# Early loads of an attention kernel: packed query and key rows, v uncast on the sync queue, weights and filter ordered behind v, sines after the first exps

## The chip, the cores and the metric

The kernel runs on one core of one Trainium2 chip. The metric is the time of one execution in microseconds (us). All times below are device times of that core. Each run carries a state: fast, slow, or unknown for a kernel that was run only once. A profiled execution has a span, which is the part that the profile covers and is 1.8 to 2.1 us shorter than the time; spans are compared with spans and times with times.

Engines are named as the profile names them: PE is TensorE, PEld its weight load, DVE is VectorE, ACT is ScalarE, POOL is GpSimd, SP is SyncE, which here only issues DMAs. "A queue" is a stream of DMA work: one is filled by GpSimd, one by the sync engine, one can be filled by ScalarE. A "piece" is one contiguous run of bytes that a DMA engine moves; 16 DMA engines work for the core.

## The reference, cut to what matters

```python
# q, k, v: (4 batches, 8 heads, 768, 64) f32, scaled by 0.1; n_global = 8, n_local = 96
scores = q @ k^T / 8
keep   = (column < 8) or (0 <= row - column < 96)
bias   = -slope[head] * (96 if global and not local else |row - column|)
a      = softmax(scores + bias, masked by keep)
x      = a @ v                       # heads joined: (4, 768, 512)
x1, x2, x3 = split(x @ w_proj)       # w_proj: (512, 1536)
y      = x1 * irfft(rfft(x2) * rfft(filter)) * x3     # over the 768 positions
out    = y @ w_out                   # w_out: (512, 512)
```

The kernel builds the Fourier transform as matmuls with cosine and sine tables. It works on four batches one after the other. Attention of batch 0 cannot overlap with the convolution of an earlier batch, because there is none; so the start of the kernel is the place where TensorE can run dry.

## The kernel before: the parts that the change and the argument touch

The kernel records its operations with a model cost, what each reads and writes, and a bias. A greedy scheduler then orders them on a modelled clock, and the result is the program order of each engine. Two things follow for the reader. An order between two operations on the same engine is real. An order between two engines is real only where data dependences make one wait for the other; the framework inserts those waits, and the scheduler's clock inserts none.

```python
def load(self, eng, dst, src, w, nbytes, name, r=()):      # G: GpSimd's queue, S: the sync queue
    self.loads += 1
    e = {"G": self.nc.gpsimd, "S": self.nc.sync}[eng]
    return self.g.op(eng, ..., lambda _: e.dma_start(dst, src),
                     w=w, r=r, nbytes=nbytes, name=name, bias=-2000.0 + self.loads)

def load_q(self, b, t):                                    # 1024 pieces of 256 B
    src = self.q[b, :, P * t:P * t + P, :].rearrange("h p d -> p h d")
    if b == 0:    # f32 by the sync queue, then a cast on VectorE
        ...
    else:         # GpSimd's queue casts on the way
        self.load("G", self.qn[:, t], src, [("qn", t)], (1024, 256), f"q{t}")

def load_v(self, b, ts):
    ...
    for t in ts:
        self.load_rows(("vn", s), vt, self.v, b, t)        # GpSimd's queue, cast on the way
        ...                                                # global rows: SBUF copies on the sync queue

# eight mask exps, one a head, 648 columns each, after the sines
for h in range(self.H):
    g.op("A", act(648), lambda _, h=h: nc.scalar.activation(
        self.mask[:, h], dm.rearrange("p a b -> p (a b)"), Act.Exp, scale=-self.slopes[h]), ...)

def load_first(self):
    for c in range(3):
        for t in ([0, 1, 2], [3, 4], [5])[c]:
            self.load_q(0, t)
        for t in self.GRP[c]:
            self.load_rows(("kn",), self.kn, self.k, 0, t)
        if c == 0:
            self.distances()
        self.load_v(0, self.GRP[c])
    ...
    for o in (0, 256):
        self.load_w(o, 256)
        self.load_w(2 * self.DM + o, 256)
    self.load_w(self.DM, self.DM)
    self.load("G", self.fl, ...)                           # the filter
```

In each attention a head pair goes through scores (PE), two exps (ACT), a mask product (DVE), and value matmuls (PE) that read v.

The softmax here doesn't subtract the row's maximum and nothing guards it: scores larger than these inputs give would overflow.

## Time and profile before

| | before |
|---|---|
| time | 200.63 us, median of 3 runs (200.32 to 201.04) |
| span of the profiled run | 198.0 us |
| TensorE busy | 185.1 us of it |
| first exp of attention 0 | 20.91 us |
| value matmuls of the second head pair (the marker used below) | 23.64 us |
| first projection with w | 32.72 us |

The page of the kernel before gives the busy time of each engine, and in 40 slices of about 5 us the busy tenths of TensorE and its granted clock.

```profile
PE 185.1 (93%) x1654; PEld 109.7 (55%) x1654; DVE 151.0 (76%) x380; ACT 150.3 (76%) x305; POOL 75.7 (38%) x96
...
PE   7993699989999699999999999999999999999992
...
PEclk9998599999999969999999999999999999999999
```

The fourth and fifth digits are the hole: TensorE is full everywhere else but for one dip near 65 us. The windows of the kernel before show it in numbers. The columns are the stretch, its length, then busy us and instruction counts of PE, PEld, DVE, ACT and POOL, then granted clock, DMA share and GB/s.

```profile
15.00:20.00 5.00, 1.79 (x19) 0.83 (x15) 1.68 (x5) 4.99 (x8) 5.00 (x7) 0.83 1.44 98
20.00:25.00 5.00, 3.54 (x40) 2.66 (x39) 3.07 (x9) 5.00 (x12) 5.00 (x7) 0.50 1.79 153
...
30.00:40.00 10.00, 9.77 (x117) 6.48 (x115) 8.67 (x21) 5.33 (x13) 4.47 (x6) 1.00 1.81 182
```

TensorE waits for ScalarE there. The timeline of ScalarE before (start, length, engine, line, operation, tiles, count) says why: an exp table load, 5.17 us of mask exps, and only then the exps of the scores.

```profile
14.54 1.28 ACT L551 ACT_TABLE_LOAD   x1
15.83 5.17 ACT L551 ACTIVATE mask<-dm 128x648 f16<-128x648 f32 x8
20.91 6.80 ACT L645 ACTIVATE E<-bank 128x432 f16<-128x432 f32 x16
```

The timeline of GpSimd before shows that v comes ahead of w on the same queue: the last three v loads are issued at 17.30 us, and w only after them.

```profile
17.30 2.65 POOL L376 DMA_DIRECT2D vn<-in_v_dram  x3
19.89 3.78 POOL L376 DMA_DIRECT2D w<-in_moe_w_proj_dram  x5
```

After the hole TensorE is what bounds the kernel.

### The profile page before, as it was taken

The numbers are of one execution on the slowest core, as the hardware profiler recorded it, in microseconds if no ns is written. First come the engines' busy times: TensorE is split into PE (matmuls) and PEld (weight loads), VectorE is DVE, ScalarE is ACT, GpSimd is POOL, SyncE is SP. The second block draws the span as 40 slices with busy tenths as digits, with TensorE's granted clock in tenths as the row PEclk, the third lists the DMA queues.
The fourth block names the chain that finished last, engine by engine and source line by source line (L and its number), as shares of the span: only waits on it lengthen the run. The fifth ranks groups of instructions, "written<-read, shape, count | busy, mean of one in ns | idle before, by whom it ended". The sixth has DMA issues, their size and how long they took to land.

```text
span 198.0 us, 4444 instructions
## 1 busy us (share of the span) xinstructions
PE 185.1 (93%) x1654; PEld 109.7 (55%) x1654; DVE 151.0 (76%) x380; ACT 150.3 (76%) x305; POOL 75.7 (38%) x96
## 2 busy tenths in 40 slices
PE   7993699989999699999999999999999999999992
PEld 2571465755545486665455657654656665445640
DVE  5993599795599999898169999951998999159540
ACT  3889997384899987387698966857999975785852
POOL 8969983499889899085000100000000000000000
PEclk9998599999999969999999999999999999999999
DMA  7999999999999999999620400025000000214025
GB/s 156 214 152 96 152 184 209 158 157 144 147 167 156 154 154 161 108 69 148 223 110 0 30 0 0 5 106 212 3 2 3 0 3 0 106 53 159 3 108 211
DMA packets 90933, 20.90 MB, mean 106 GB/s; under 512 B 83776, under 2 KB 87840, under 8 KB 90912
## 3 DMA queue, kind: packets, MB, share of 16 engines
q0 software_dynamic: 80912, 12.52, 95.7%
q1 hardware_dynamic: 10000, 8.10, 12.6%
q8 instruction: 13, 0.21, 0.4%
q14 instruction: 8, 0.07, 0.1%
HBM read 26.61 MB, written 6.29 MB: 166 GB/s over the span
## 4 chain that ended last, share of the span: by engine, by line
PE 72%; DMA 10%; POOL 9%; DVE 4%; issue 2%; ACT 1%; POOLq 0%; ACTq 0%
PE bank L739 19%; PE bank L786 11%; PE bank L826 10%; PE bank L595 8%; PE bank L806 8%; DMA kn<-in_k_dram 5%; DMA w<-in_moe_w_proj_dram 5%; PE bank L633 4%; PE bank L677 3%; POOL vn L376 3%; PE bank L608 3%; PE bank L712 3%; POOL kn L376 3%; PE bank L682 2%; POOL w L376 1%
## 5 line engine op out<-in xcount | busy, mean ns | idle before, releaser
L739 PE MATMUL bank<-xT,w 128*128 128x384 f16 x256 | 44.1, 326 | 0.1
L645 ACT ACTIVATE E<-bank 128x432 f16<-128x432 f32 x96 | 42.7, 570 | 0.5 <-PE bank L633 0.3
L376 POOL DMA_DIRECT2D kn<-in_k_dram x28 | 25.2, 915 | 23.5 <-PE bank L608 17.8
L739 PEld LDWEIGHTS <-w 128*128 128x128 f16 x256 | 24.8, 98 | 16.9
L376 POOL DMA_DIRECT2D vn<-in_v_dram x28 | 25.2, 922 | 6.4 <-PE bank L682 5.2
L364 ACT ACTIVATE x<-bank 128x384 f16<-128x384 f32 x31 | 15.7, 508 | 15.4 <-PE bank L739 14.3
L656 DVE TENSOR_TENSOR E<-E,mask 128x864 f16<-128x864 f16 x32 | 18.6, 602 | 7.6 <-ACT E L645 7.3
L697 DVE TENSOR_TENSOR xn<-bank,rc 128x256 f16<-128x256 f32 (+1 forms) x48 | 22.5, 469 | 1.7
L826 PE MATMUL bank<-wo,y 128*128 128x512 f16 x96 | 22.4, 379 | 0.0
L747 DVE TENSOR_TENSOR g<-bank,x 128x384 f16<-128x384 f32 x32 | 17.3, 552 | 5.6 <-PE bank L739 5.2
L364 ACT ACTIVATE ot<-bank 128x512 f32<-128x512 f32 x24 | 14.3, 597 | 8.8 <-PE bank L826 8.8
L360 ACT CAST eo<-bank 128x384 f16<-128x384 f32 x31 | 14.7, 487 | 7.2 <-PE bank L806 6.8
L677 PE MATMUL bank<-vn,E 128*128 128x65 f16 x224 | 19.6, 201 | 0.1
L677 PEld LDWEIGHTS <-E 128*128 128x128 f16 x224 | 16.3, 103 | 4.9 <-DVE E L656 1.3
L682 PE MATMUL bank<-vn,E 128*128 128x65 f16 x192 | 19.1, 199 | 0.0
L806 PE MATMUL bank<-inv,X 128*128 128x384 f16 x96 | 18.7, 326 | 0.0
L595 PE MATMUL bank<-ab,fwd 128*128 128x512 f16 x72 | 18.3, 379 | 0.0
L376 POOL DMA_DIRECT2D qn<-in_q_dram x18 | 16.0, 913 | 2.2 <-PE bank L633 0.7
L633 PE MATMUL bank<-QT,KT 64*128 64x216 f16 (+2 forms) x224 | 15.9, 248 | 0.7 <-DVE inv L360 0.2
L608 PE MATMUL bank<-ident,kn 128*128 128x128 f16 x112 | 10.9, 231 | 5.8 <-ACT E L645 4.4
L682 PEld LDWEIGHTS <-E 128*128 128x128 f16 x192 | 14.7, 101 | 1.2
L826 PEld LDWEIGHTS <-y 128*128 128x128 f16 x96 | 9.4, 98 | 10.5
(103 smaller groups left out, 323.3 us busy)
## 6 DMA issues: line engine op xcount, KB each, us to landing
out_dram<-ot SPq DMA_DIRECT2D x24, 256.0 KB
kn<-in_k_dram POOLq DMA_DIRECT2D x24, 128.0 KB, 5.7
vn<-in_v_dram POOLq DMA_DIRECT2D x24, 128.0 KB, 6.2
qn<-in_q_dram POOLq DMA_DIRECT2D x18, 128.0 KB, 7.8
ot<-in_q_dram SPq DMA_DIRECT2D x6, 256.0 KB
w<-in_moe_w_proj_dram POOLq DMA_DIRECT2D x4, 256.0 KB, 6.5
g<-in_moe_filter_fft_dram POOLq DMA_DIRECT2D x1, 768.0 KB, 12.9
w<-in_moe_w_proj_dram POOLq DMA_DIRECT2D x1, 512.0 KB, 9.4
```

The source lines that it names most:

```text
L364: self.nc.scalar.mul(out, in_, c)
L376: return self.g.op(eng, 0.57 + 0.00035 * nbytes[0] if eng == "G" else 0.5, lambda _: e.dma_start(dst, src), w=w, r=r, nbytes=nbytes, name= ...
L595: self.nc.tensor.matmul(b.f32(), self.fwd[:, kt, s, :], src[i][:, kt, :], start=(kt == 0), stop=(kt == 2))
L633: nc.tensor.matmul(bs[hh].f32()[:, off:off + w], self.KT[hs, hp, P * m:P * m + P], self.QT[hs, hp, KL * m:KL * m + w], start=(off == 0), s ...
L645: g.op("A", act(432), lambda _, hh=hh: nc.scalar.activation(eo[:, hh], bs[hh].f32()[:, 0:432].rearrange("p (m w) -> p m w", m=2), Act.Exp, ...
L677: nc.tensor.matmul(o[:, hh, i], ef[:, at:at + P], vt[:, t, 2 * hp + hh, :], start=first, stop=(t == 0), skip_group_check=True)
L682: nc.tensor.matmul(o[:, hh, i], ef[:, at:at + P], vt[:, t - 1, 2 * hp + hh, :], start=False, stop=True, skip_group_check=True)
L697: nc.vector.tensor_mul(xn[:, ts[0]:ts[0] + nt].rearrange("p t h d -> p h t d"), o[:, :, :, 0:D], r.to_broadcast([P, 2, nt, D]))
L739: nc.tensor.matmul(bk.f32()[:, 0:h], self.w[:, c, o + P * j:o + P * j + P], self.xT[:, c, h * s:h * s + h], start=(c == 0), stop=(c == 3))
L786: nc.tensor.matmul(bk.f32(), src[:, c, P * t:P * t + P], w[:, c, DM:2 * DM], start=(c == 0), stop=(c == 3))
L806: nc.tensor.matmul(bk.f32()[:, 0:h], X[:, s, cs], self.inv[:, s, :], start=(s == slots[0]), stop=(s == slots[-1]))
L826: nc.tensor.matmul(bk.f32(), y[:, c, P * t:P * t + P], self.wo[:, c, :], start=(c == 0), stop=(c == 3))
```

## The change

The intent is to start attention 0 sooner. Queries and keys of batches 0 and 1 are loaded by head pair as six consecutive rows per partition: for the queries of a batch, four loads of 256 pieces of 1536 B in place of six loads of 1024 pieces of 256 B. w goes out in three loads in place of five. The masks are computed from 264 columns a head and spread by copies, in place of exps over 648. The sines, and their table load, go behind the first exps. v of batch 0 goes out uncast on the sync queue, into memory that is free at that time, and seven casts on ScalarE and VectorE bring it into place; the intent is to keep it apart from GpSimd's queue. The loads of w, of the filter and of batch 1 are declared as readers of v tiles, so that they come "behind v". The diff, cut to its core:

```diff
 def load_first(self):
-        for c in range(3):
-            for t in ([0, 1, 2], [3, 4], [5])[c]:
-                self.load_q(0, t)
-            for t in self.GRP[c]:
-                self.load_rows(("kn",), self.kn, self.k, 0, t)
-            if c == 0:
+        for hp in range(4):
+            self.load_pair("q", 0, hp)
+            self.load_pair("k", 0, hp)
+            if hp == 1:
                 self.distances()
-            self.load_v(0, self.GRP[c])
 ...
-        for o in (0, 256):
-            self.load_w(o, 256)
-            self.load_w(2 * self.DM + o, 256)
-        self.load_w(self.DM, self.DM)
+        self.first_v()
+        for o in (0, 2 * self.DM, self.DM):
+            self.load_w(o, self.DM, [("vn", 0, 4)])
         self.load("G", self.fl, ..., (768, 2048), "filter",
+                  [("vn", 0, 6)])

+    def first_v(self):
+        ...
+        for t in range(7):
+            st, ks = ...                       # a free buffer: h1, h2 or X, read as f32
+            for rows, n, src in ((slice(0, NG), NG, 0), (slice(NG, P), KL, self.K0[t])):
+                self.load("S", st[rows], self.v[0, :, src:src + n].rearrange("h p d -> p h d"),
+                          [("vst", t, n)], (8 * n, 256), f"v{t}")
+            g.op("AV", ..., lambda e, st=st, t=t: self.copy(e, vt[:, t, :, 0:self.D], st), ...,
+                w=[("vn", 0, t)], name="vcast")

+    def load_pair(self, what, b, hp):          # 256 pieces of 1536 B
+        hs = slice(2 * hp, 2 * hp + 2)
+        src = (self.q if what == "q" else self.k)[b, hs].rearrange("h (p t) d -> p h (t d)", t=6)
+        ...
+            self.load("G", self.packed(what)[:, hs], src, [(what + "p", hp)] + ..., (256, 1536), ...)

-        for h in range(self.H):
-            g.op("A", act(648), ...)           # a mask exp a head
+        for hp in range(4):
+            for h in (2 * hp, 2 * hp + 1):
+                for lo, hi, at in ((0, n, n), (n, n + 48, 600)):   # 216 and 48 columns
+                    g.op("A", act(hi - lo), ...)
+            ...                                # VectorE copies spread them

 def graph(self):
         self.setup()
-        self.tables()
         self.load_first()
         self.attention(0)
+        g.batch = (-10.0, 0.0)
+        self.tables()
 # cut: the transposes of packed rows, the distances, the scheduler's model of two DMA queues
```

## The prediction

> **What bounds the kernel now.** The engine summary has TensorE busy 185.1 of 198.0 us. By the busy-time windows it is dense from about 32 us to the end at a granted clock near 1.0; before that it is starved (1.79 us busy in 15 to 20, 3.54 in 20 to 25). In the timeline the first exp starts at 20.9 us, behind the distance mask (Pool until 14.7 us) and eight mask exps on ScalarE (5.17 us from 15.83). The chain of waits then runs through the w load (9.4 us, to 32.3) and a key load of batch 1 (9.9 us). The change acts on the start; my marker is the value matmuls of the second head pair (23.6 us). About 174 us follow it.
>
> **What it removes.** Query and key loads of batches 0 and 1 fall from 1024 pieces of 256 B to 256 of 1536 B per load. Mask exps fall from 648 to 264 columns a head (estimate 3.5 us for 5.2); sines leave the start. Without v, exps could begin near 13 us.
>
> **What it adds.** v of batch 0 goes to the SP queue uncast: 7168 pieces of 256 B, then seven casts (about 0.5 us each). Packed batch 1 needs 48 half-width transposes each for q and k, not 24 and 28: some 2 us of TensorE. A sine and an exp table load (1.28 us each) move into the middle.
>
> **The step that decides.** "Held behind v" is an order in the schedule's model only. In the instruction order Pool issues the three w loads without any wait, right after the `far` selects and one key load; the filter and batch 1 follow, waiting only for old slots and transposes. I expect w issued at 10 to 13 us and a Pool backlog from about 13 to 43 us, beside v on SP's queue. The Trainium skill, "DMA: Bandwidth & Descriptors", section on queues, rings and completion order, says each DMA engine alternates between queues packet by packet. The DMA packet records agree: alone, SP moves 1000 pieces of 256 B per us; [...]at 28.6 to 29.4 us SP's 1040 B pieces come every 0.14 us, one per 2 KB of w. So v gets about one 256 B piece per 2048 B w piece or 1536 B q/k piece on each engine (94 and 77 ns a pair, estimates from those rates). Then v tiles 0 and 1 land by 14 us, 2 about 20, 3 about 27, 4 about 33, 5 about 38, 6 about 46. The casts sit in order on ScalarE ahead of the exps (tiles 1 to 4) and on VectorE ahead of the first mask products (5, 6), so all of attention 0 waits.
>
> **Sum.** Marker 23.6 to about 47 us (+23); minus about 5 for weights and batch 1 already there, plus about 3 for transposes, tables and a cold clock: +18 to +21. Predicted 219 us, range 203 to 229. Chances: faster 0.15, same 0.09, slower 0.76.
>
> **What would show it.** In the timeline, w issued before 13 us; v casts ending long idle stretches on ScalarE and VectorE between 14 and 47 us; TensorE nearly empty there, dense after; w landed by 25 us.
>
> **What would make it wrong.** If the queues share by time or SP is favoured, v is in by about 24 us, attention 0 starts some 8 us sooner than before, and the time is 188 to 195. If Pool issues w late, v escapes most of the contention.

## The result, and the profile after

The changed kernel takes 224.91 us (median of 4 runs, 222.81 to 225.07), beside 200.8 us of the kernel before in the same rounds. The ratio is 1.118, with a 95% interval of 1.111 to 1.125. Here and below a ratio is the mean time of one kernel's fast runs over that of the other's of the same rounds, so it is not quite the ratio of the medians quoted. The prediction (slower, 219 us, range 203 to 229) was right.

The page after gives the same three lines as before.

```profile
PE 184.9 (83%) x1715; PEld 106.9 (48%) x1715; DVE 152.9 (68%) x390; ACT 156.8 (70%) x326; POOL 57.8 (26%) x79
...
PE   7590001129999999979999999999999999999993
...
PEclk9998555556999999999999999999999999999998
```

TensorE does the same amount of work (184.9 us beside 185.1). All that is new is a longer hole: six slices of about 5.6 us each are empty or nearly so. The windows after show it, in the columns explained above.

```profile
15.00:20.00 5.00, 1.63 (x34) 1.04 (x31) 3.55 (x15) 0.00 (x0) 2.91 (x4) 1.00 1.26 195
20.00:25.00 5.00, 0.54 (x4) 0.30 (x5) 2.31 (x8) 1.85 (x5) 1.28 (x2) 0.56 1.22 197
25.00:30.00 5.00, 0.00 (x0) 0.00 (x0) 1.48 (x5) 0.85 (x2) 0.82 (x2) 0.50 1.23 195
30.00:40.00 10.00, 1.42 (x11) 0.79 (x11) 0.00 (x0) 2.21 (x4) 4.78 (x6) 0.50 1.24 183
```

From 20 to 40 us no compute engine is busy for half of the time. Only the DMA works throughout, at 183 to 197 GB/s; before it was 98 and 153 GB/s in the first two of these stretches. The clock has fallen to 0.50, as "TensorE: Matmul & The Clock Gate" of the Trainium skill says in its Part 1 (the default state is throttled, and activity releases it); this trace agrees, with a mean of 0.50 from 25 to 50 us and 0.77 from 50 to 60. The low clock is a consequence here and not the cause: in the stretch from 25 to 30 us TensorE ran no instruction.

What the engines wait for is v. The waits view after, for the first 60 us (line, what it waited for, total us, times, longest us), begins with two lines:

```profile
DVE vn L366 <- DMA h<-in_v_dram: 24.4, 2, 19.3
ACT vn L366 <- DMA h<-in_v_dram: 23.2, 4, 7.8
```

The timelines after name the casts one by one. In brackets is the idle time before each and what ended it. ScalarE first, then VectorE:

```profile
21.62 0.62 ACT L366 CAST vn<-h 128x512 f16<-128x512 f32 x1 [7.80 <-DMA h<-in_v_dram]
29.14 0.62 ACT L366 CAST vn<-h 128x512 f16<-128x512 f32 x1 [5.67 <-DMA h<-in_v_dram]
35.84 0.62 ACT L366 CAST vn<-h 128x512 f16<-128x512 f32 x1 [5.38 <-DMA h<-in_v_dram]
...
41.90 0.62 ACT L366 CAST vn<-h 128x512 f16<-128x512 f32 x1 [4.31 <-DMA h<-in_v_dram]
```

```profile
45.78 0.43 DVE L366 CAST vn<-h 128x512 f16<-128x512 f32 x1 [19.31 <-DMA h<-in_v_dram]
46.13 0.60 DVE L735 TENSOR_TENSOR E<-E,mask 128x864 f16<-128x864 f16 x1
...
48.55 0.43 DVE L366 CAST vn<-X 128x512 f16<-128x512 f32 x1 [1.73 <-DMA X<-in_v_dram]
48.89 0.60 DVE L735 TENSOR_TENSOR E<-E,mask 128x864 f16<-128x864 f16 x1
```

Each engine runs in order, so a cast that waits for its tile holds the exps and mask products behind it, although these need no v. The value matmuls of the second head pair are the marker. The timelines of TensorE before and after:

```profile
23.64 0.29 PE L677 MATMUL bank<-vn,E 128*128 128x65 f16 x2
```

```profile
49.55 0.29 PE L756 MATMUL bank<-vn,E 128*128 128x65 f16 x2 [1.78 <-DVE E L735]
```

The marker moved by 25.9 us and the span by 25.2 us (223.2 beside 198.0). From the marker to the end it is 174.4 us before and 173.7 us after. So the whole loss is in the start.

v comes late because it shares the DMA engines with loads that the change meant to hold back. The timeline of GpSimd after, with nothing in brackets: no wait stands before w or the filter.

```profile
7.95 0.89 POOL L382 DMA_DIRECT2D kn<-in_k_dram  x1
8.83 2.24 POOL L382 DMA_DIRECT2D w<-in_moe_w_proj_dram  x3
11.04 0.86 POOL L382 DMA_DIRECT2D g<-in_moe_filter_fft_dram  x1
```

The queue view after, from 17 to 22 us, gives packets, MB (as written) and the share of engine time of each queue; q0 is GpSimd's, q1 the sync queue. Below it is the same view of the kernel before from 5 to 6 us, when both queues moved pieces of 256 B.

```profile
q0 software_dynamic: 795, 0.79, 93.6%
q1 hardware_dynamic: 695, 0.17, 26.7%
```

```profile
q0 software_dynamic: 908, 0.11, 170.7%
q1 hardware_dynamic: 275, 0.07, 34.1%
```

(The counts hold some packets of 4 bytes; the shares of overlapping packets add up to more than 100%.) After, the two queues take turns nearly piece by piece, 795 to 695, while a w piece is 2048 B read (1024 B written) and a v piece 256 B. v gets some 140 pieces per us from 17 to 28 us. The 908 to 275 of the kernel before is no ratio of turns, because the view adds up engines: from 5.2 to 5.6 us the records hold 39 sync pieces beside 406 of GpSimd's queue, and by their start times (the records name no engine) these 39 are only a few chains, some with a piece every 14 ns (about the pace of an engine that has sync pieces alone) and some with one every 39 ns. A count from the trace's DMA packet records, by size and microsecond, gives these rates (pieces per us, all 16 engines):

```
kernel and stretch            GpSimd's queue                      sync queue
before, 3 to 4 us             nothing                             256 B: about 1050
after, 17 to 22 us            2048 B read: about 155              256 B: about 135
after, 32 to 36 us            1536 B read: about 175              256 B: about 180
e1 (below), 13 to 15 us       256 B read, cast: about 394         256 B: about 387
```

The start times of one queue's pieces repeat with a step of 105 ns beside 2048 B, 86 ns beside 1536 B and 39 ns beside cast pieces of 256 B, and the other queue's pieces repeat with the same step where it was looked for (2048 B and 256 B). With 16 engines, these steps would make 152, 186 and 410 pairs per us, close to the counts: one piece of each queue in turn.

### The profile page after: what moved, and what is told of

It reads as the page before. It is cut to its first block, busy times and chain, and to the rows that moved or that the text cites. A ratio compares the mean times of both kernels' runs of the same rounds, so it can differ in the third digit from the quotient of the medians.

```text
span 223.2 us, 4576 instructions
## 1 busy us (share of the span) xinstructions
PE 184.9 (83%) x1715; PEld 106.9 (48%) x1715; DVE 152.9 (68%) x390; ACT 156.8 (70%) x326; POOL 57.8 (26%) x79
## 4 chain that ended last, share of the span: by engine, by line
PE 62%; SPq 16%; DVE 7%; ACT 6%; DMA 5%; issue 2%; DVEq 0%; ACTq 0%
PE bank L818 18%; SPq L382 16%; PE bank L910 9%; PE bank L870 9%; PE bank L634 7%; PE bank L890 5%; DMA X<-in_v_dram 5%; PE bank L710 3%; PE bank L756 3%; ACT E L723 2%; PE bank L791 2%; PE bank L761 2%; DVE E L735 2%; DVE xn L776 2%; PE bank L685 2%
## 5 line engine op out<-in xcount | busy, mean ns | idle before, releaser
L723 ACT ACTIVATE E<-bank 128x432 f16<-128x432 f32 x96 | 43.5, 556 | 4.9 <-PE bank L710 3.2
L710 PE MATMUL bank<-QT,KT 64*128 64x216 f16 (+2 forms) x224 | 17.2, 265 | 24.9 <-ACT QT L366 19.5
L382 POOL DMA_DIRECT2D vn<-in_v_dram x21 | 18.8, 897 | 51.7 <-PE bank L761 36.6
L710 PEld LDWEIGHTS <-KT 64*128 64x128 f16 x224 | 8.9, 99 | 32.9 <-issue 24.3
L756 PE MATMUL bank<-vn,E 128*128 128x65 f16 x224 | 19.0, 198 | 4.5 <-DVE E L735 4.5
L382 POOL DMA_DIRECT2D kn<-in_k_dram x22 | 18.9, 861 | 13.9 <-PE bank L685 5.8
L756 PEld LDWEIGHTS <-E 128*128 128x128 f16 x224 | 15.7, 100 | 11.0 <-DVE E L735 7.2
L366 ACT CAST vn<-h 128x512 f16<-128x512 f32 x4 | 2.5, 620 | 23.2 <-DMA h<-in_v_dram 23.2
L761 PE MATMUL bank<-vn,E 128*128 128x65 f16 x192 | 18.4, 196 | 0.0
L366 DVE CAST vn<-h 128x512 f16<-128x512 f32 x2 | 0.9, 454 | 24.4 <-DMA h<-in_v_dram 24.4
L382 POOL DMA_DIRECT2D qn<-in_q_dram x16 | 14.1, 879 | 13.5 <-DMA w<-in_moe_w_proj_dram 5.0
```

The lines of the kernel that those rows point to most:

```text
L382: return self.g.op(eng, 0.57 + 0.00035 * nbytes[0] if eng == "G" else 0.5, lambda _: e.dma_start(dst, src), w=w, r=r, nbytes=nbytes, name= ...
L710: nc.tensor.matmul(bs[hh].f32()[:, off:off + w], self.KT[hs, hp, P * m:P * m + P], self.QT[hs, hp, KL * m:KL * m + w], start=(off == 0), s ...
L723: g.op("A", act(432), lambda _, hh=hh: nc.scalar.activation(eo[:, hh], bs[hh].f32()[:, 0:432].rearrange("p (m w) -> p m w", m=2), Act.Exp, ...
L756: nc.tensor.matmul(o[:, hh, i], ef[:, at:at + P], vt[:, t, 2 * hp + hh, :], start=first, stop=(t == 0), skip_group_check=True)
L761: nc.tensor.matmul(o[:, hh, i], ef[:, at:at + P], vt[:, t - 1, 2 * hp + hh, :], start=False, stop=True, skip_group_check=True)
```

## The experiments

Nine kernels were run. Theory A: v of batch 0 is starved on the sync queue beside the large loads of GpSimd's queue, because nothing makes w wait for v; nothing else in the change costs much. Rivals: the loss comes from another part of the change (more transposes, later sines, packed rows, casts), or it is due to how the scheduler remade the order of everything else. Five kernels keep the changed kernel's order of compute on every engine (e1, e3, e4, e6, e9); they change only DMAs, waits and how many rows a cast covers. Three (e2, e5, e7) let the scheduler make a new order. b1 starts from the kernel before, and its order is new too.

### b1_vsp: the kernel before, with only v of batch 0 moved

```diff
 # kernel before, load_first
-            self.load_v(0, self.GRP[c])
+            self.first_v(self.GRP[c])     # as in the changed kernel: uncast, sync queue, then a cast a tile
```

> The kernel before with one part of the change alone: v of batch 0 uncast on SP's queue with seven casts; q, k, masks, sines and the order of loads stay. Theory A: this part alone makes the loss. SP's queue holds q and v (256 B pieces) beside Pool's k, w, filter and batch 1 (256 B pieces[...]); v's last cast at 45 to 60 us, time 222 to 245 us. Rival C (the loss needs the packed loads or the late sines): below 208 us.

It measured 220.75 us in its one run (state unknown), just under the 222 to 245 us that I expected and far from rival C's 208, beside a median of 199.7 us of the kernel before on the same chip. In the windows of b1, TensorE is nearly empty at half clock, and its last v cast, in the timeline of VectorE, comes at 43.53 us.

```profile
20.00:30.00 10.00, 2.47 (x15) 0.94 (x14) 3.08 (x8) 3.56 (x8) 2.63 (x3) 0.50 1.29 190
30.00:40.00 10.00, 2.87 (x26) 2.00 (x26) 2.04 (x5) 0.49 (x2) 3.57 (x4) 0.50 1.59 165
```

```profile
43.53 0.43 DVE L360 CAST vn<-X 128x512 f16<-128x512 f32 x1 [1.22 <-DMA X<-in_v_dram]
```

With this part of the change alone the loss is about 21 us. The last cast came 1.5 us sooner than expected. The scheduler's order is new in this kernel, and the later query tiles now stand behind v on the sync queue (the timeline of VectorE has a query cast at 32.75 us, after 5.39 us of waiting for its load). So b1 tells which part costs and not every microsecond of it; e1 and e9 have to show the cause.

### e1_hold: the changed kernel, with w and the filter really held behind v

```diff
+        t = {"w0": 4, "filter": 6}.get(name)
+        def start(_):
+            if t is not None:              # GpSimd first copies one element of the cast v tile into the destination
+                first = self.w[0:1, 0, 0:1] if name == "w0" else self.fl[0:1, 0, 0:1]
+                self.nc.gpsimd.tensor_copy(first, self.vn[0][0:1, t, 0, 0:1])
+            e.dma_start(dst, src)
```

> The changed kernel in the same instruction order on every engine, but with a real hold: before the first w load Pool copies one element of v tile 4 (batch 0), before the filter load one of v tile 6, so that w, filter and batch 1 are issued only after those casts. Theory A (v starves because each DMA engine alternates one 256 B piece of v with one 2 KB piece of the Pool queue): v runs nearly alone at about 1000 pieces per us, the last v cast falls from 48.6 us to about 20, the value matmuls of the second head pair come at about 21 to 22 us, and the time falls from 224.9 to 194 to 202 us. Rival B (v is slow by itself: small uncast pieces on SP, and SP's issues waiting for old semaphore slots): the last v cast stays beyond 40 us and the time stays above 215. Rival C (packed transposes and late sines cost the bulk): v is early but the time stays above 212.

It measured 201.41 us (median of 4, 200.8 to 201.85), beside 199.86: ratio 1.0064, interval 1.0019 to 1.0109. The timeline of GpSimd in e1 shows the hold, that of VectorE the last v cast, and that of TensorE the marker:

```profile
22.56 0.23 POOL L387 COPY w<-vn 1x1 f16<-1x1 f16 x1 [13.72 <-ACT vn L366]
23.09 2.24 POOL L388 DMA_DIRECT2D w<-in_moe_w_proj_dram  x3 [0.30 <-POOL w L387]
```

```profile
23.69 0.42 DVE L366 CAST vn<-X 128x512 f16<-128x512 f32 x1
```

```profile
25.50 0.29 PE L763 MATMUL bank<-vn,E 128*128 128x65 f16 x2
```

A wait put in, and nothing taken out, gave back 23.5 us of the loss (224.91 to 201.41, medians of different rounds). v then moved 450 to 1030 pieces per us between 15 and 22 us by the packet records, with no piece of w moving. That is theory A, and it excludes rivals B and C (above 215 and above 212 us). But the last cast came later than expected, at 23.69 us, and the kernel is no faster than before.

### e6_land: the hold put on the landing of v in place of its cast

```diff
 # against e1
-                self.nc.gpsimd.tensor_copy(first, self.vn[0][0:1, t, 0, 0:1])
+                self.nc.gpsimd.tensor_copy(first, st[32:33, 0, 0:1])     # st: the f32 buffer of tile t
```

> The held kernel (first run, 201.4 us), with the hold on the landing of v tiles 4 and 6 in their staging buffers instead of on their casts, which came 3 us after the landing; same instruction order. w should be issued at 18 to 19 us instead of 23.1 and land 4 us sooner, v still complete by 23 us since w's first bytes come some 2 us after its issue. Theory A plus the reading that the held kernel is then bound by when w and batch 1 arrive: 197 to 200 us. If the arrival of w and batch 1 does not matter: 201 to 202.

It measured 200.89 us (median of 4, 200.48 to 201.54), beside 199.7: ratio 1.0062, interval 1.0022 to 1.0102. It lies between the two expectations (197 to 200, and 201 to 202). w went out 2.1 us sooner than in e1 (21.02 beside 23.09 us; I had expected 18 to 19), and little or nothing came of it.

```profile
21.02 2.24 POOL L390 DMA_DIRECT2D w<-in_moe_w_proj_dram  x3 [0.30 <-POOL w L389]
```

The marker says why: it stands at 25.71 us, later than before (23.64), because the order still has the casts of v ahead of the exps, and by the packet records v alone takes until about 22 us to arrive on the sync queue.

### e9_vbody: v cast by GpSimd's queue ahead of w, everything else in the changed kernel's order

```diff
+        def start(_):
+            if name == "w0":                                   # seven loads of 960 pieces, ahead of w
+                for i in range(7):
+                    lo = self.K0[i]
+                    e.dma_start(self.vn[0][NG:P, i, :, 0:self.D],
+                                self.v[0, :, lo:lo + KL].rearrange("h p d -> p h d"))
+            if name[0] == "v" and eng == "S" and nbytes[0] == 8 * KL:
+                return                                         # the sync queue keeps the 8 global rows
+            e.dma_start(dst, src)
 ...
-                e, vt[:, t, :, 0:self.D], st), ...
+                e, vt[0:NG, t, :, 0:self.D], st[0:NG]), ...    # a cast of 8 rows stays in each cast's place
```

> The changed kernel with its own order of compute on every engine, except that the 120 local rows of each v tile are cast by GpSimd's queue (seven loads of 960 pieces of 256 B, issued just ahead of the first w load) straight into place. The 8 global rows of each tile stay uncast on the sync queue, and the seven casts stay where they are but only touch those 8 rows. Theory A (v starved behind w, and nothing else, costs the time): w is issued at about 15 us, all of v is in by about 18 us, the last v cast is by 20 us, and the time is 194 to 201 us, at or a little under the kernel before. Rival D (the changed kernel loses something of its own in the later stages or by casting v on GpSimd, which the run with the remade schedule showed as 206.0 us): 204 to 208 us here too.

It measured 198.18 us (median of 6, 197.26 to 199.45), beside 200.2: ratio 0.9921, interval 0.9875 to 0.9966. That is inside what theory A expected, and rival D's 204 to 208 is excluded. (v itself arrived later than I expected: by the packet records its last pieces moved at 21.8 us and not by 18.) Timelines of GpSimd, VectorE and TensorE in e9:

```profile
8.84 6.46 POOL L386 DMA_DIRECT2D vn<-in_v_dram  x7
15.29 2.41 POOL L390 DMA_DIRECT2D w<-in_moe_w_proj_dram  x3
```

```profile
20.18 0.41 DVE L366 CAST vn<-X 8x512 f16<-8x512 f32 x1
```

```profile
21.16 0.23 PE L765 MATMUL bank<-vn,E 128*128 128x65 f16 x2 [0.29 <-DVE E L744]
```

This version beats both kernels, by 0.8% (the interval excludes 1) and by 12%. The rest of the change is thus a small gain, once v does not have to share. Its marker comes 2.5 us before that of the kernel before. The kernel before, the changed one and three with the changed kernel's order can be put side by side; the last column is the span less the marker.

| kernel | marker, us | span, us | marker to end, us |
|---|---|---|---|
| before | 23.64 | 198.0 | 174.4 |
| after | 49.55 | 223.2 | 173.7 |
| e1_hold | 25.50 | 199.7 | 174.2 |
| e6_land | 25.71 | 199.3 | 173.6 |
| e9_vbody | 21.16 | 195.8 | 174.6 |

What follows the marker takes 173.6 to 174.6 us in all of them, whether w and batch 1 came early (after) or late (e1).

### e3_split: two of the seven v tiles on ScalarE's queue

```diff
+        if eng == "S" and name in ("v1", "v3"):
+            e = self.nc.scalar
```

> The changed kernel, same order on PE, DVE and Pool, but v tiles 1 and 3 are issued on ScalarE's queue and the other five on SP's, so that v has two queues beside Pool's. Theory A: a round is then one Pool piece and two v pieces (about 110 ns against 94 for half as many v pieces); the 144 pieces per engine on the extra queue cost 16 ns each and not 94, so the last v tile lands about 11 us sooner (cast at 36 to 39 us against 48.6) and the time is about 11 us less, 212 to 216. Rival B1 (shares go by bytes or by time between hardware and software queues, however many): last v cast stays at 46 to 49 us, time 222 to 226. Rival B2 (SP's issue chain is the limit): v is faster than A says for the tiles on ScalarE, but SP's five tiles keep a pace of about 6 us each.

It measured 219.36 us in one run (state unknown); its last cast, in the timeline of VectorE, came at 42.88 us in place of 48.55.

```profile
42.88 0.43 DVE L366 CAST vn<-X 128x512 f16<-128x512 f32 x1 [4.69 <-DMA X<-in_v_dram]
```

The direction is right and the size is half of what I expected (212 to 216). At 11 us three queues have work, and the packet records count 149 pieces of GpSimd's queue, 131 v pieces of the sync queue and 150 of ScalarE's in that microsecond: a third queue is a third turn. But tiles 1 and 3 were through by 17 us, when w had only just begun to flow, and from there v had one turn again. "DMA: Bandwidth & Descriptors" of the Trainium skill says under "Rules for kernel authors" that spreading DMAs over issuing engines does not help bandwidth and only saves issue time. This run roughly agrees for the sum (the windows from 8 to 17 us give 216 GB/s beside 204 in the changed kernel); but for one stream beside another the number of queues changed its share.

### e4_w1k: w in pieces half as long

```diff
+            if name in ("w0", "w512", "w1024"):
+                for i in (0, 256):
+                    e.dma_start(dst[:, :, i:i + 256], src[:, :, i:i + 256])   # 1024 B read a piece, not 2048
```

> The changed kernel, same order on PE, ACT and DVE, with w loaded in pieces of 1024 B (six loads of 256 columns) instead of 2048 B (three loads). If a Pool packet is some 2 KB whatever its pieces (theory A as predicted): two w pieces pass for each v piece, v keeps about 140 to 160 pieces per us while w runs and its landings and the time stay within 1.5 us of the changed kernel's. If the alternation is piece by piece: while w runs (about 12 us) v gets about twice as many pieces per us, about 270, so v gains some 1500 pieces, and the last v tile lands 5 to 8 us sooner, time about 217 to 220.

It measured 223.28 us in one run (state unknown), which is within the changed kernel's own 222.81 to 225.07, with the last v cast at 46.97 us, 1.6 us sooner than in the changed kernel. From 20 to 25 us the packet records count about 225 w pieces and about 220 v pieces per us. So the turns go piece by piece with pieces of 1024 B too; v's rate beside w rose from about 140 to 220 per us, and w took twice as many turns for the same bytes. Neither expectation was met exactly: the rates are those of turns piece by piece, the time and the last cast are nearer to the other case. The records show where the gain went: at 28 us v was about 1000 pieces ahead of the changed kernel (4340 beside 3344) and at 44 us still 860, but the last 125 pieces took until about 47 us; why they were so slow stays open. My reading in the prediction, one v piece "per 2 KB of w", is therefore not a rule about 2 KB: it is one piece of each, at every length seen here.

### e2_vpool: v back on GpSimd's queue, order remade by the scheduler

```diff
-        self.first_v()
+        self.load_v(0, range(7))      # as before: GpSimd's queue, cast on the way, ahead of w
```

> The changed kernel with one part undone: v of batch 0 again on the Pool queue, cast by the load, ahead of w; all else stays (packed q and k, sines late), and the schedule is made anew. Theory A: no second queue, no starvation; v's last tile lands at about 17 us, the second head pair's value matmuls come near 18 us, w is in by about 25 us, time 190 to 198 us, so below before. Rival B: also about that, since SP is not used. Rival C: above 212 us.

It measured 231.1 us: ratio 1.1531, interval 1.1467 to 1.1594. A miss, and not one about v. The waits view of e2, for the first 60 us, has this line:

```profile
PE bank L650 <- DMA qn<-in_q_dram: 25.8, 3, 20.0
```

The new order put batch 1's packed query load ahead of the query transposes of batch 0. The packed load of pair 0 declares that it overwrites pair 0's key and the unpacked tiles, but not the other pairs of batch 0 that lie in the same memory, so the scheduler was free to do so. The transposes then waited for a load that they did not want, and read queries of the wrong batch. The result was still reported as correct. A likely reason, argued and not tested, is that q and k are scaled by 0.1, so that the scores are close to zero beside the bias. In the changed kernel's own order this does not happen, but the fault is latent in it.

### e5_vpool2: the same, with that dependence mended

```diff
+                f"{what}{b}{hp}", late, [x for x in self.g.ops if x.name == "q"] if what == "q" else ())
 # batch 1's packed q loads come after all four query transposes of batch 0
```

> The second run again (v of batch 0 on the Pool queue, cast by the load, ahead of w), mended: there the new schedule had put batch 1's first packed q load, which lies over all head pairs of batch 0's q, ahead of batch 0's transposes, which then waited 20 us for it and read the wrong q. Now each of these loads waits for all of batch 0's q transposes. Theory A: one queue, nothing starves; v lands between 13 and 20 us, w between 20 and 29, the second head pair's value matmuls come at 18 to 21 us (23.6 before, 48 to 49 in the changed kernel), time 193 to 199 us. Rival C (packed transposes, later sines and table loads cost more than the packed loads bring): 201 us or more.

It measured 206.0 us (205.69 to 206.23): ratio 1.0318, interval 1.0276 to 1.0361. Most of the loss is gone, but my 193 to 199 was missed, and the time falls where rival C had put it (201 or more). The exps started at 16.59 us, so v and the masks were early enough. The timeline of TensorE in e5 shows what the value matmuls then waited for:

```profile
26.14 0.24 PE L756 MATMUL bank<-vn,E 128*128 128x65 f16 x1 [1.93 <-DMA vn<-vn]
```

That DMA is a copy of v's global rows on the sync queue. The new order also runs the scores and all 24 exps of attention 0 in one go, from 16.59 to 26.84 us. From 26.14 us to the end it is 177.5 us here, some 3 us more than in the table above (the marker is not quite the same one, as the order differs), so the remade order costs later too. When this run came in I took it as evidence that v on GpSimd's queue might cost something of its own; e9, which has no new order, rules that out for the 120 local rows of each tile, and rules out rival C for the changed kernel's own order. The copy of the global rows is not in e9.

### e7_pack0: e5 with batch 1 unpacked

```diff
-    PACKED = {("q", 0), ("k", 0), ("q", 1), ("k", 1)}
+    PACKED = {("q", 0), ("k", 0)}
```

> As the first kernel of this call, but batch 1's q and k in tiles of 256 B pieces as before; only batch 0 is packed. If packing batch 1 is worth its transposes: batch 1's q and k come about 3 us later and the time is 1 to 3 us above that kernel. If its 44 extra half-width transposes (some 2 us of TensorE) cost more: the time is 1 to 2.5 us below it.

It measured 214.44 us: ratio 1.0759, interval 1.0698 to 1.082. It missed the expected 3 us around e5. The waits view of e7, for the first 80 us, begins with GpSimd held by one load:

```profile
POOL kn L382 <- PE bank L685: 16.5, 1, 16.5
```

A load of a later batch waits there for TensorE at the head of GpSimd's queue, and all loads behind it wait too. The order was remade once more, so this run says nothing reliable about what packing batch 1 is worth. That stays open.

## Why the prediction was right, point by point

- "Held behind v" is an order in the schedule's model only: right. w was issued at 8.83 us without a wait (I expected 10 to 13). e1 made the hold real and recovered the loss, which shows the cause.
- v starved by taking turns with longer pieces: right. e9 shows that undoing this part alone is enough for the cure, and b1 (one run, order remade) that it is enough for a loss of the same size.
- The size of a turn was too small. I worked out 94 ns a pair beside w and 77 ns beside q and k. From the rates measured (16 engines over 140 and 180 pieces per us) it is 114 and 89 ns, from the spacing of the pieces 105 and 86 ns. v tiles 1 to 5 were cast at 21.6, 29.1, 35.8, 41.9 and 45.8 us where I had landings at 14, 20, 27, 33 and 38; the last was cast at 48.55 where I had 46.
- Most of that delay was not the size of a turn: tile 1 was already 7.6 us late, and after it the steps of 7.5, 6.7 and 6.1 us are close to the 6, 7 and 6 that I had. By the packet records 674 v pieces had moved by 12 us and 1129 by 14, while I needed two whole tiles (2048) by 14. Until then v shared with the packed key loads (from 11 to 12 us, 200 of their pieces and 119 of v), while the prediction has GpSimd's backlog begin at about 13 us. The end was faster than I had it (353 and 357 v pieces per us from 44 to 46 us, beside batch 1's cast pieces). So that the last tile came within 2.6 us of the forecast is in part luck: a late start and a fast end cancelled.
- The marker: 47 predicted, 49.55 measured. This is the first of the terms that make 219 into 225.
- "Minus about 5 for weights and batch 1 already there, plus about 3 for transposes, tables and a cold clock": this step failed in its size. The two together came to -0.7 us (174.4 to 173.7 from the marker on). The table shows that early weights are worth about nothing: with w issued at 8.83 us (after) and at 21.02 (e6) the rest takes 173.7 and 173.6 us, with a granted clock of 0.74 and 0.69 in the 10 us after the marker. TensorE is dense after the marker, so there was almost no idle time left to give back.
- The sum: +25.9 for the marker and -0.7 for the rest make +25.2 us of span, where I had +18 to +21. The direction and the mechanism were right; the size was 4 to 7 us short.
- w "landed by 25 us": the last of three landed at about 27 us (issued at about 10.3, 17.0 us to landing). A small miss, of the same origin as the turns.
- The counter-case of the prediction (v in early would give 188 to 195 us) was too bright. With v on the sync queue and in by about 22 us, e1 and e6 take 201.41 and 200.89 us; with v early and the same order, e9 gives 198.18 us. In e9 the start moved by 2.5 us and not by 8, while ScalarE was already full with casts and masks: 4.82 of the 5 us from 10 to 15 in the windows of e9, with the first exp at 16.91 us.

What stays open is the worth of each remaining part (packed rows, short masks, late sines); only their sum was measured, 0.8% in e9.

## What to carry to other kernels

An order in a scheduler's clock is not a wait: look in the instruction stream for what actually holds a DMA back, and if nothing does, assume that it starts at once. When two queues share the DMA engines, a stream of short pieces got about one piece for each long piece of the other queue here, so put the short pieces that are needed first on the same queue ahead of the long ones, or make the long ones wait on data. To test one part of a change in a kernel whose order is made by a scheduler, keep the order fixed; three runs with a remade order missed their expectations for reasons that had nothing to do with the question.

## What the Trainium skill lacked or had wrong

- "DMA: Bandwidth & Descriptors", section "Queues, rings and completion order", says that each DMA engine goes round its queues by whole packets, typically 9 to 17 descriptors. The runs show about one piece of each queue in turn beside pieces of 2048 B, 1536 B, 1024 B and 256 B read (about 155 to 135, 175 to 180, 225 to 220 and 394 to 387 per us), and 149 : 131 : 150 with three queues. Turns of many pieces were not seen.
- The same section does not say what this means for a stream of short pieces: 256 B pieces fell from about 1050 per us alone to about 140 beside pieces of 2048 B.
- "DMA: Bandwidth & Descriptors", section "Rules for kernel authors": spreading over issuing engines "only saves sequencer issue time". In e3 it also changed the share of one stream beside another, and the last v tile was cast at 42.88 us in place of 48.55 (one run).
